# A decode step with attention and a gated MLP: 4 MB loads of keys and values in four large slots

## The chip, the cores and the metric

The kernel runs on one core of a Trainium2 chip. Five engines work side by side, each through its own list of instructions in order: TensorE (PE in the profile, its weight loads PEld), VectorE (DVE), ScalarE (ACT), GpSimd (POOL) and SyncE (SP). They meet only through semaphores. SBUF is the memory on the core, with 128 partitions; PSUM takes the results of matmuls. Sixteen DMA engines move data between HBM and SBUF; a load is issued by an engine, here nearly always SP, and is split into packets over the sixteen.

The metric is device time in microseconds of one execution. Before the change three runs gave 127.43 to 127.46 us, median 127.45.

## The reference

One token, a row x of 576 numbers, goes through two branches in parallel. x is layer-normalised first, and the result is x + A + B.

```python
# A: attention over the last W = 4096 positions of a cache of 65536
q = (xn @ wq)                      # 32 query heads of 128
k, v = k_cache[..., -W:, :], v_cache[..., -W:, :]   # 16 heads, each serves two query heads
p = softmax(q @ k.T * 128 ** -0.5)
A = (p @ v).reshape(1, 4096) @ wo
# B: gated MLP, sequence length 1
z = gelu(xn @ w_in)                # 4608
g = w_sp * layernorm(z[2304:]) + b_sp
B = (z[:2304] * g) @ w_out
```

All data are bfloat16. With one query row, nearly all of the work is to read memory: 33.6 MB of keys and values, and 4.7, 5.3, 2.7 and 4.7 MB of wq, w_in, w_out and wo: 50.96 MB.

## The kernel before, in words

**Loads.** All large loads are issued by SP, in the order of the program, into a ring of seven slots of 20736 bytes per partition (pool `ring`, L60; the loads L83, L90 and L95). There are 28: wq in three pieces of 1, 2 and 1.5 MB, w_in in three, eight loads of keys and eight of values, each for two heads (2 MB, 16 KB per partition, L90), w_out in one, wo in five (14, 9, 6, 2 and 1 rows per partition). A load into a used slot waits on SP until the last reader of the slot is done, and everything behind it on SP waits as well. Keys run two loads ahead of values.

**Layout of a key load.** A partition holds a run of consecutive positions of one head. For the scores q·k the 128 components of a key must lie along the partitions, so VectorE transposes 32x32 blocks of 32-bit words (`t_half`, L262, the transposes at L268) into a tile kT; one load is two halves of 2 transposes each. The blocks do not bring components alone onto the partitions but pairs of bf16 in a word and remainders of the position; the matmul takes out one component group at a time by reading kT with a step.

**Scores.** `s_half` (L271, matmul at L277) does 8 matmuls of 512 columns per half: for each of two heads four (`be` = 0 to 3) that accumulate in PSUM. Each head has its own tile position, a strip of 32 columns of the array, so matmuls of different positions can run at the same time. Within kT a head's successive columns lie 4 elements apart.

**Groups.** Four heads make a group; there are four groups. The loop at the end runs over 16 halves, four per group. In the last half of a group come `sm_a` (L296: maximum over the scores, spread over partitions, then two exponentials of 64 partitions x 1024 columns on ScalarE at L305) and pv of the group before (L338, matmul at L344: 32 matmuls of 512 columns over four positions). In the second half of the next group comes `sm_b` (L309: two transposes of the exponentials on VectorE at L315, sixteen copies of 32 x 64 words on ScalarE at L321 into the tile PT that pv reads). `norm` (L351), `y_mms` and `y_copy` turn the result of pv into four columns of Y; they follow one group later still. The MLP's `z_mms` (L375), gelu and layer norm are put between the halves of groups 0 and 1.

**The end.** After the loop: the last `sm_b`, pv, then 24 of the 36 matmuls with w_out, which need nothing of attention, then norm and Y of the last group, the other 12, and the 64 matmuls with wo (L467). A copy on VectorE and one on ScalarE and a small store end the kernel.

The order on every engine is that of the program: the kernel switches automatic scheduling off (L70), so an engine waits where an instruction stands that is not ready, even if a later one is. Semaphores for slots, PSUM tiles and buffers are put in by the framework.

Of the kernel before, what the change touches and what calls it, by code (L numbers as in the profile page):

```python
# [22 lines left out]
NT = W // 128  # L23
GK = 4
NG = HKV // GK
NP = HKV // 2
TP = 2 * NT
# [6 lines left out]
RING = 7  # L34
NS = 9
SLOT = NF * D
# [3 lines left out]
def kernel(  # L40
# [19 lines left out]
    ring = ctx.enter_context(tc.tile_pool(name="ring", bufs=RING))  # L60
    const = ctx.enter_context(tc.tile_pool(name="const", bufs=1))
    work = ctx.enter_context(tc.tile_pool(name="work", bufs=2))
    ktpool = ctx.enter_context(tc.tile_pool(name="ktpool", bufs=3))
# [11 lines left out]
    def ring_tile(name, rows, width):  # L75
        t = ring.tile([P, SLOT], BF16, name=name, tag="ring")
        return t[:, 0:rows * width].rearrange("p (s c) -> p s c", c=width)

    def load_halves(src, lo, n, name):

        v = ring_tile(f"{name}{lo}", n, src.shape[1] // 2)
        rows = src.rearrange("r (e c) -> (r e) c", e=2).rearrange("(p s) c -> p s c", s=NS)
        nc.sync.dma_start(v, rows[:, lo:lo + n, :])  # L83
        return [(lo + s, v[:, s, :]) for s in range(n)]

    def load_kv(src, m, name):

        t = ring.tile([P, SLOT], BF16, name=f"{name}{m}", tag="ring")
        v = t[:, 0:TP * DH]
        nc.sync.dma_start(v, src[0, 2 * m:2 * m + 2, SK - W:SK, :].rearrange("h (r t) d -> r h (t d)", t=TP))  # L90
        return v.rearrange("p (t d) -> p t d", d=DH)

    def load_n(src, per, lo, n, name):
        v = ring_tile(f"{name}{lo}", n, D)
        nc.sync.dma_start(v, src.rearrange("(p t) n -> p t n", t=per)[:, lo:lo + n, :])  # L95
        return [(lo + t, v[:, t, :]) for t in range(n)]

    K, V = {}, {}
    wq_sb = load_halves(A_wq, 0, 2, "wq") + load_halves(A_wq, 2, 4, "wq") + load_halves(A_wq, 6, 3, "wq")
    for m in range(2):  # L100
        K[m] = load_kv(A_k_cache, m, "k")
    win_sb = sum((load_halves(B_w_in, lo, 3, "win") for lo in (0, 3, 6)), [])
    for m in range(2, NP):
        K[m] = load_kv(A_k_cache, m, "k")
        V[m - 2] = load_kv(A_v_cache, m - 2, "v")
    for m in range(NP - 2, NP):
        V[m] = load_kv(A_v_cache, m, "v")
    wout_sb = load_n(B_w_out, NF, 0, NF, "wout")
    wo_sb = []
    for n in (14, 9, 6, 2, 1):  # L110
        wo_sb += load_n(A_wo, 32, len(wo_sb), n, "wo")
# [28 lines left out]
    idv = ident[:].rearrange("p (q c hh) -> p q c hh", q=4, hh=4)[:, :, 0:4, :]  # L140
    cm = const.tile([P, 4], FP32, name="cm")
    nc.vector.tensor_reduce(out=cm[:], in_=idv.rearrange("p q c hh -> p c q hh"), op=ALU.add,
                            axis=mybir.AxisListType.XY)
    dmask = const.tile([P, 4, DH], FP32, name="dmask")
    nc.gpsimd.tensor_copy(dmask[:], cm[:].unsqueeze(2).to_broadcast([P, 4, DH]))
    ohm = const.tile([P, 2, 4], FP32, name="ohm")
    for pr in range(2):
        nc.vector.tensor_reduce(out=ohm[:, pr, :], in_=idv[:, 2 * pr:2 * pr + 2].rearrange("p q c hh -> p hh q c"),
                                op=ALU.add, axis=mybir.AxisListType.XY)
# [3 lines left out]
    selv = sel[:].rearrange("p q (r hh e) -> p q r hh e", r=2, hh=4)  # L153
    for dq in range(4):
        nc.gpsimd.tensor_copy(selv[:, dq, :, :, dq], ohm[:])

    ids = ident[:].rearrange("p (i a h) -> p i a h", i=4, h=2)[:, :, 0:4, :]
    oha = const.tile([P, 4, 2], FP32, name="oha")
    nc.vector.reduce_sum(oha[:], ids.rearrange("p i a h -> p i h a"), axis=AXX)

    lsum = const.tile([P, 4, 8, 2, 2], FP32, name="lsum")
    nc.gpsimd.memset(lsum[:], 0.0)
    for hd in range(2):
        for pr in range(2):
            for th in range(2):
                nc.gpsimd.tensor_copy(lsum[:, 2 * pr + th, 0:4, hd, :],
                                      oha[:, 2 * hd + pr, :].unsqueeze(1).to_broadcast([P, 4, 2]))

    pz = []
    for n in range(2):  # L170
        t = const.tile([P, TP, 16, 2], BF16, name=f"pz{n}")
        nc.gpsimd.memset(t[:], 0.0)
        pz.append(t)
# [88 lines left out]
    def t_half(m, hf):  # L262

        kT = ktpool.tile([P, NT, 2, 16, 2, 2], BF16, name=f"kT{m}_{hf}", tag="kT")
        src = K[m][:, NT * hf:NT * (hf + 1), :].rearrange("p t d -> p (t d)").bitcast(FP32)
        dst = kT[:].rearrange("p t b r x e -> p (t b r x e)").bitcast(FP32)
        for n in range(2):
            nc.vector.transpose(dst[:, 1024 * n:1024 * (n + 1)], src[:, 1024 * n:1024 * (n + 1)])  # L268
        KT[m, hf] = kT

    def s_half(m, hf):  # L271
        g, pr = divmod(m, 2)
        kv = KT.pop((m, hf))[:].rearrange("p t b r x e -> p b e x t r")
        for hd in range(2):
            i = 2 * hd + pr
            for be in range(4):
                nc.tensor.matmul(  # L277
                    S[g % 2][32 * i:32 * i + 8, hf, :],
                    lhsT=Qb[:, 2 * m + hd, be].rearrange("p a h -> p (a h)"),
                    rhs=kv[:, be // 2, be % 2, hd],  # L280
                    start=(be == 0), stop=(be == 3), tile_position=(0, 32 * i),
                )
# [13 lines left out]
    def sm_a(g):  # L296
        s = S[g % 2]
        nc.vector.tensor_reduce(out=mx[:, 0:1], in_=s[:], op=ALU.max, axis=mybir.AxisListType.XY)  # L298
        bk = spread(mx, mb, g, ALU.max, "m")
        nm = work.tile([P, 1], FP32, name=f"nm{g}", tag="nm")  # L300
        nc.vector.tensor_scalar_mul(nm[:], bk[:, 0:1], -SCALE)  # L301
        p = pz[g % 2]
        for hd in range(2):
            lo, hi = 64 * hd, 64 * hd + 64
            nc.scalar.activation(p[lo:hi, :, :, hd], s[lo:hi].rearrange("p a (t r) -> p (a t) r", r=16), ACT.Exp,  # L305
                                 bias=nm[lo:hi, 0:1], scale=SCALE, accum_out=lx[lo:hi, g:g + 1])
        st[g] = {"p": p}

    def sm_b(g):  # L309
        d = st[g]  # L310
        pt = work.tile([P, TP, 32], BF16, name=f"pt{g}", tag="pt")
        src = d["p"][:].rearrange("p t r x -> p (t r x)")
        dst = pt[:].rearrange("p t x -> p (t x)")
        for n in range(2):
            nc.vector.transpose(dst[:, 1024 * n:1024 * (n + 1)], src[:, 1024 * n:1024 * (n + 1)])  # L315
        PT = work.tile([P, 2, TP, 2, 2], BF16, name=f"PT{g}", tag="PT")
        pt4 = pt[:].rearrange("p t x -> p (t x)").bitcast(FP32).rearrange("p (t x) -> p t x", x=16)
        PT4 = PT[:].rearrange("p r t x h -> p (r t x h)").bitcast(FP32).rearrange("p (r t x) -> p r x t", r=2, x=2)
        for i in range(GK):
            for a in range(4):  # L320
                nc.scalar.copy(PT4[32 * a:32 * a + 32, i % 2, i // 2, :], pt4[32 * i:32 * i + 32, :, a])  # L321
        d["PT"] = PT

    def sums(g):

        lps = ps_m.tile([P, 32], FP32, name=f"lps{g}", tag="m")
        nc.tensor.matmul(lps[:, 0:1], lhsT=lsum[:].rearrange("p q c x h -> p (q c x h)"), rhs=lx[:, g:g + 1],  # L327
# [10 lines left out]
    def pv(g):  # L338

        d = st[g]  # L340
        for tb in range(NT // 4):
            for q in range(4):
                pr, t0 = q // 2, NT * (q % 2) + 4 * tb
                nc.tensor.matmul(  # L344
                    ops[32 * q:32 * q + 16, :],
                    lhsT=d["PT"][:, pr, t0:t0 + 4].rearrange("p t x h -> p (t x h)"),
                    rhs=V[2 * g + pr][:, t0:t0 + 4, :],
                    start=(tb == 0), stop=(tb == NT // 4 - 1), tile_position=(0, 32 * q),
# [79 lines left out]

    for j in range(2 * NP):
        g, o = divmod(j, GK)  # L430
        t_half(j // 2, j % 2)
        if o == 3:
            if g > 0:
                recip(g - 1)
            if g > 1:
                norm(g - 2)
        s_half(j // 2, j % 2)
        if g > 0 and o == 1:
            if g > 1:
                sm_b(g - 1)  # L440
            else:
                G, sz = z_gelu(*z_exp(zps))

                acc = []
                for n, pool in enumerate((ps_a, ps_b)):
                    t = pool.tile([P, 512], FP32, name=f"acc{n}", tag="ab"[n])
                    acc.append(t[32 * n:32 * n + 1, 0:CW])
                    nc.tensor.matmul(acc[n], lhsT=ones_b[:, 0:1], rhs=xrow[:, CW * n:CW * (n + 1)],
                                     start=True, stop=False, tile_position=(0, 32 * n))
                hv = z_norm(G, sz)  # L450
        if g > 0 and o == 2:
            sums(g - 1)
        if o == 3:
            if g > 1:
                y_mms(g - 2)
            sm_a(g)
            if g > 1:
# [67 lines left out]
```

## Time and profile before

| what | value |
|---|---|
| median of 3 runs | 127.45 us (127.43 to 127.46) |
| span of the profiled execution | 125.4 us; no other time of that execution is given |
| TensorE busy | 68.4 us in 626 matmuls |
| VectorE busy | 78.5 us in 150 instructions |
| ScalarE busy | 33.6 us in 85 instructions |
| GpSimd busy | 7.9 us |
| moved by DMA | 51.06 MB in 4047 packets, 407 GB/s over the span |

The page cuts the span into 40 slices of about 3.1 us and gives, for each engine, the busy tenth of each slice, the clock that TensorE was granted (5 is half speed), and the busy share of the DMA engines. The chain that ended last is followed back from the last instruction to whatever released each wait. A group's line has the source line, engine, operation, output<-input with their shapes, the count, and then busy time, mean ns of one, and the idle time of the engine before it with what ended it. A line of the timeline has start, duration, engine, line, operation and count. Durations of overlapping matmuls are longer than the distance of their starts; where matmuls at four positions overlap, the distance is what counts.

### The profile page before, as it was taken

What the parts mean: (1) busy time and instruction counts of PE and PEld (TensorE: products, weight loads), DVE (VectorE), ACT (ScalarE), POOL (GpSimd) and SP (SyncE); (2) the same over time, 40 slices, a digit from 0 to 9 for tenths busy, and PEclk for the clock granted to TensorE, in tenths of its full rate; (3) what the DMA queues carried; (4) which work ended last, traced back from release to release, by engine and by line L of the source; (5) the groups of instructions that cost most, each with busy time, mean ns of one, the idle gap of its engine ahead of it and who ended that gap; (6) DMA issues with size and microseconds to landing.
All of it is one profiled execution on the core that took longest, in us unless ns stands there. A gap on an engine that the chain in (4) does not pass through costs nothing.

```text
span 125.4 us, 1630 instructions
## 1 busy us (share of the span) xinstructions
PE 68.4 (55%) x626; PEld 31.4 (25%) x626; DVE 78.5 (63%) x150; ACT 33.6 (27%) x85; POOL 7.9 (6%) x27
## 2 busy tenths in 40 slices
PE   0034810398999668069257049639029811178862
PEld 0021110112699612014011012411003511024640
DVE  6853049997517595794798298899098967005001
ACT  4000030000072950000441940260860092920001
POOL 2991000000000000100000000000000000000000
PEclk9999995558975555959958977986955996557998
DMA  4999999999999999999999999999999999999960
GB/s 115 455 423 422 425 434 439 422 428 435 428 438 418 434 434 428 423 444 423 428 439 434 413 439 434 428 428 434 428 436 434 428 426 439 434 409 427 416 261 0
DMA packets 4047, 51.06 MB, mean 407 GB/s; under 512 B 454, under 2 KB 584, under 8 KB 840
## 3 DMA queue, kind: packets, MB, share of 16 engines
q1 hardware_dynamic: 4032, 50.96, 95.6%
q8 instruction: 5, 0.08, 0.2%
q14 instruction: 2, 0.02, 0.0%
q10 hardware_dynamic: 8, 0.00, 0.0%
HBM read 50.96 MB, written 0.00 MB: 406 GB/s over the span
## 4 chain that ended last, share of the span: by engine, by line
DMA 71%; PE 11%; DVE 11%; issue 2%; SPq 1%; ACT 1%
DMA k<-in_A_k_cache_dram 44%; DMA wo<-in_A_wo_dram 17%; DMA wq<-in_A_wq_dram 10%; DVE kT L268 6%; PE S L277 5%; PE ops L344 3%; DVE Qb L255 2%; PE qps L227 1%; PE acc L467 1%; DVE q_rep L238 1%; ACT q_rep L236 1%; DVE on L358 1%; PE lps L327 1%; SPq L83 1%; DVE om L354 1%
## 5 line engine op out<-in xcount | busy, mean ns | idle before, releaser
L277 PE MATMUL S<-kT,Qb 128*8 128x512 bf16 x128 | 32.3, 636 | 30.3 <-DVE kT L268 30.3
L268 DVE STREAM_TRANSPOSE kT<-k 128x1024 f32<-128x1024 f32 x32 | 36.9, 1212 | 8.3 <-DMA k<-in_A_k_cache_dram 8.3
L305 ACT ACTIVATE pz<-S,nm 64x1024 bf16<-64x1024 f32 x8 | 11.2, 1406 | 45.0 <-DVE nm L301 30.3
L321 ACT COPY PT<-pt 32x64 f32<-32x64 f32 x64 | 18.9, 295 | 14.6 <-DVE pt L315 13.8
L277 PEld LDWEIGHTS <-Qb 128*8 128x8 bf16 x128 | 6.4, 96 | 49.7 <-issue 46.7
L344 PE MATMUL ops<-v,PT 128*16 128x512 bf16 x128 | 11.7, 441 | 3.5 <-ACT PT L321 3.5
L315 DVE STREAM_TRANSPOSE pt<-pz 128x1024 bf16<-128x1024 bf16 x8 | 9.4, 1212 | 4.1 <-ACT pz L305 4.1
L380 PEld LDWEIGHTS <-win 128*128 128x128 bf16 x162 | 10.1, 165 | 0.9 <-issue 0.9
L380 PE MATMUL zps<-XT,win 128*128 128x2 bf16 x162 | 10.2, 201 | 0.0
L354 DVE SCALAR_TENSOR_TENSOR om<-ops,rs,dmask 128x512 f32<-128x512 f32 x4 | 3.0, 742 | 7.4 <-PE ops L344 7.3
L298 DVE TENSOR_REDUCE mx<-S 128x1 f32<-128x1024 f32 x4 | 4.9, 1220 | 3.7 <-PE S L277 3.7
L344 PEld LDWEIGHTS <-PT 128*16 128x16 bf16 x128 | 5.0, 97 | 7.3 <-ACT PT L321 4.1
L227 PE MATMUL qps<-wq,XT 128*2 128x512 bf16 x36 | 4.2, 621 | 2.3 <-DVE XT L218 1.9
L467 PE MATMUL acc<-wo,Y 128*1 128x288 bf16 x64 | 4.6, 285 | 1.3 <-DMA wo<-in_A_wo_dram 1.3
L236 ACT CAST q_rep<-qps 128x512 bf16<-128x512 f32 x2 | 1.2, 585 | 14.0 <-DVE q_rep L238 14.0
L238 DVE CAST q_rep<-qps 128x512 bf16<-128x512 f32 x2 | 1.4, 692 | 5.1 <-PE qps L227 4.5
L193 PE MATMUL ps_x<-ones_b,xtw 1*128 1x1 bf16 x9 | 0.4, 162 | 7.2 <-DVE xtw L191 7.2
L492 DVE CAST res<-acc 1x288 bf16<-1x288 f32 x1 | 0.4, 446 | 6.1 <-PE acc L467 6.1
L358 DVE TENSOR_REDUCE on<-om 128x128 f32<-128x512 f32 x4 | 4.1, 1034 | 0.1
L327 PE MATMUL lps<-lx,lsum 128*128 128x1 f32 x8 | 2.1, 333 | 3.2 <-DVE Y L372 3.2
L493 ACT CAST res<-acc 1x288 bf16<-1x288 f32 x1 | 0.4, 389 | 12.4 <-PE acc L467 12.4
L467 PEld LDWEIGHTS <-Y 128*1 128x1 bf16 x64 | 2.9, 83 | 3.0 <-issue 1.9
(90 smaller groups left out, 46.8 us busy)
## 6 DMA issues: line engine op xcount, KB each, us to landing
k<-in_A_k_cache_dram SPq DMA_DIRECT2D x8, 2048.0 KB, 27.2
v<-in_A_v_cache_dram SPq DMA_DIRECT2D x8, 2048.0 KB, 27.8
win<-in_B_w_in_dram SPq DMA_DIRECT2D x3, 1728.0 KB, 27.1
wout<-in_B_w_out_dram SPq DMA_DIRECT2D x1, 2592.0 KB, 30.2
wq<-in_A_wq_dram SPq DMA_DIRECT2D x1, 2048.0 KB, 9.3
wo<-in_A_wo_dram SPq DMA_DIRECT2D x1, 2016.0 KB
wq<-in_A_wq_dram SPq DMA_DIRECT2D x1, 1536.0 KB, 12.5
wo<-in_A_wo_dram SPq DMA_DIRECT2D x1, 1296.0 KB
```

The source lines that it names most:

```text
L227: nc.tensor.matmul(qps[32 * g:32 * g + 2, :], lhsT=XT[:, s, :], rhs=wv[:, 512 * g:512 * (g + 1)], start=(s == 0), stop=(s == NS - 1), tile ...
L268: nc.vector.transpose(dst[:, 1024 * n:1024 * (n + 1)], src[:, 1024 * n:1024 * (n + 1)])
L277: nc.tensor.matmul(S[g % 2][32 * i:32 * i + 8, hf, :], lhsT=Qb[:, 2 * m + hd, be].rearrange("p a h -> p (a h)"), rhs=kv[:, be // 2, be % 2 ...
L298: nc.vector.tensor_reduce(out=mx[:, 0:1], in_=s[:], op=ALU.max, axis=mybir.AxisListType.XY)
L305: nc.scalar.activation(p[lo:hi, :, :, hd], s[lo:hi].rearrange("p a (t r) -> p (a t) r", r=16), ACT.Exp, bias=nm[lo:hi, 0:1], scale=SCALE, ...
L315: nc.vector.transpose(dst[:, 1024 * n:1024 * (n + 1)], src[:, 1024 * n:1024 * (n + 1)])
L321: nc.scalar.copy(PT4[32 * a:32 * a + 32, i % 2, i // 2, :], pt4[32 * i:32 * i + 32, :, a])
L344: nc.tensor.matmul(ops[32 * q:32 * q + 16, :], lhsT=d["PT"][:, pr, t0:t0 + 4].rearrange("p t x h -> p (t x h)"), rhs=V[2 * g + pr][:, t0:t ...
L354: nc.vector.scalar_tensor_tensor(out=om[:].rearrange("p c d -> p (c d)"), in0=ops[:], scalar=d["rs"][:, 0:1], in1=dmask[:].rearrange("p c ...
L358: nc.vector.reduce_sum(on[:], om[:].rearrange("p c d -> p d c"), axis=AXX)
L380: nc.tensor.matmul(zps[:, :, t], lhsT=wt[:, t, :], rhs=XT[:, s, :], start=(s == 0 and t == 0), stop=(s == NS - 1 and t == NF - 1), skip_gr ...
L467: nc.tensor.matmul(acc[n], lhsT=lhs[:, col:col + 1], rhs=wv[:, CW * n:CW * (n + 1)], start=False, stop=last, tile_position=(0, 32 * n))
```

## The change

Keys and values come four heads at a time, a whole group in one load of 4 MB, 32 KB per partition. There are 17 loads instead of 28, into four slots named a, b, c and d of 32 KB per partition, plus a small one, f, for the last row of wo. The order of the loads on SP is wq (8 of its 9 rows per partition), wq's last row, K0, w_in (7 of 9), w_in's last two, K1, K2, V0, K3, V1, V2, V3, w_out, wo in 18, 10, 3 and 1 rows. Which slot each takes is written in the calls.

With four heads in a load, a chunk (`keys`, `scores`) is half of a group: four transposes, then 16 matmuls of 512 columns over four tile positions. Within kT a head's successive columns now lie 8 elements apart. The exponentials are four per group, each of 32 partitions x 1024 columns. The transposes of the exponentials work on 32-bit words, and the sixteen copies move 32 x 128 words each. The tiles pz and pt have one buffer instead of two. The order of the work is written as a sequence of calls: pv, norm and Y of a group follow directly after one another (`tail`), one group after its exponentials, and all 36 matmuls with w_out stand after the last `tail`.

```diff
-RING = 7
 NS = 9
-SLOT = NF * D
...
+    def load_kv(slot, src, g, name):
+
+        t = big.tile([P, TP * DH], BF16, name=f"{name}{g}", tag=slot)
+        nc.sync.dma_start(t[:], src[0, GK * g:GK * g + GK, SK - W:SK, :].rearrange("h (r t) d -> r h (t d)", t=TP))
+        return t[:].rearrange("p (t d) -> p t d", d=DH)
...
+    rest = big.tile([P, TP * DH], BF16, name="rest", tag="d")
+    wq_sb = rows("a", wq_h, "wq", 0, 8) + rows(rest, wq_h, "wq", 8, 1, 0)
+    K[0] = load_kv("b", A_k_cache, 0, "k")
+    win_sb = rows("c", win_h, "win", 0, 7) + rows(rest, win_h, "win", 7, 2, 2048)
+    K[1] = load_kv("a", A_k_cache, 1, "k")
+    K[2] = load_kv("b", A_k_cache, 2, "k")
+    V[0] = load_kv("c", A_v_cache, 0, "v")
+    K[3] = load_kv("d", A_k_cache, 3, "k")
+    V[1] = load_kv("a", A_v_cache, 1, "v")
+    V[2] = load_kv("b", A_v_cache, 2, "v")
+    V[3] = load_kv("c", A_v_cache, 3, "v")
+    wout_sb = rows("a", B_w_out, "wout", 0, NF)
+    wo_sb = (rows("d", A_wo, "wo", 0, 18) + rows("b", A_wo, "wo", 18, 10)
+             + rows("c", A_wo, "wo", 28, 3) + rows("f", A_wo, "wo", 31, 1))
...
-        kT = ktpool.tile([P, NT, 2, 16, 2, 2], BF16, name=f"kT{m}_{hf}", tag="kT")
+        kT = ktpool.tile([P, TC, 2, 8, GK, 2], BF16, name=f"kT{g}_{c}", tag="kT")
...
+    def scores(g, c):
+        kv = KT.pop((g, c))[:].rearrange("p t b r x e -> p b e x t r")
+        for be in range(4):
+            for x in range(GK):
                 nc.tensor.matmul(
+                    S[g % 2][32 * x:32 * x + 8, c, :],
+                    lhsT=Qb[:, GK * g + x, be].rearrange("p a h -> p (a h)"),
+                    rhs=kv[:, be // 2, be % 2, x],
+                    start=(be == 0), stop=(be == 3), tile_position=(0, 32 * x),
                 )
...
+        pv_ = pz[:].rearrange("p t r x e -> p t e r x")
+        for x in range(GK):
+            lo, hi = 32 * x, 32 * x + 32
+            nc.scalar.activation(pv_[lo:hi, :, :, :, x], s[lo:hi].rearrange("p a (t e r) -> p (a t) e r", e=2, r=8),
+                                 ACT.Exp, bias=nm[lo:hi, 0:1], scale=SCALE, accum_out=lx[lo:hi, g:g + 1])
...
-                nc.scalar.copy(PT4[32 * a:32 * a + 32, i % 2, i // 2, :], pt4[32 * i:32 * i + 32, :, a])
+                nc.scalar.copy(PT4[32 * a:32 * a + 32, :, x, :], pt[32 * x:32 * x + 32, :, 2 * a:2 * a + 2])
...
+    def group(g, between):
+        keys(g, 0)
+        scores(g, 0)
+        between()
+        keys(g, 1)
+        scores(g, 1)
+        sm_a(g)
+
+    group(0, lambda: None)
+    zps = z_mms()
+    sm_b(0)
+    zg = []
+    group(1, lambda: zg.extend(z_exp(zps)))
+    G, sz = z_gelu(*zg)
...
+    hv = z_norm(G, sz)
+    sums(0)
+    group(2, lambda: sm_b(1))
+    pv(0)
+    tail(0)
+    sums(1)
+    group(3, lambda: sm_b(2))
+    pv(1)
+    tail(1)
+    sums(2)
+    sm_b(3)
+    pv(2)
+    tail(2)
+    sums(3)
+    pv(3)
...
+    tail(3)
+    for c in range(3):
+        out_hv(c)
     for t, wv in wo_sb:
         out_mms(Y, t, wv, t == 31)
```

`tail(g)` is recip, norm, y_mms and y_copy of group g; `rows` loads a number of rows of a matrix into a slot.

## The prediction

> **What bounds the kernel now.** I read the strip of slices and the chain that ended last, then the transfers, then the timeline of the last 25 us, then the rates of single instructions.
>
> ```profile
> span 125.4 us, 1630 instructions
> ...
> DMA  4999999999999999999999999999999999999960
> ...
> DMA 71%; PE 11%; DVE 11%; issue 2%; SPq 1%; ACT 1%
> ...
> wo<-in_A_wo_dram SPq DMA_DIRECT2D x1, 144.0 KB, 8.7
> ```
>
> All 16 DMA engines are busy from slice 1 to slice 38, and 71% of the chain is transfers. So the reader should see a kernel bound by its 50.96 MB. The third wq load is issued at 1.62 us and lands 12.45 us later (the chain's piece "DMA wq"), after 4.72 MB. The last load is issued at 113.88 and lands 8.7 us later, at 122.6, after 50.96 MB. Between them lie 46.24 MB in 108.5 us, 426 GB/s, and a load that ends at X MB lands at 3.0 + X/0.426 us. The three runs have a median of 127.45 us; of the profiled execution only the span is given, so 2.05 us is taken to lie around it.
>
> How late is the arithmetic behind that? The timeline of the last group:
>
> ```profile
> 100.32 1.40 ACT L305 ACTIVATE pz<-S,nm 64x1024 bf16<-64x1024 f32 x1 [7.30 <-PE ops L344]
> ...
> 101.79 1.39 ACT L305 ACTIVATE pz<-S,nm 64x1024 bf16<-64x1024 f32 x1
> ...
> 103.26 2.37 DVE L315 STREAM_TRANSPOSE pt<-pz 128x1024 bf16<-128x1024 bf16 x2 [1.00 <-ACT pz L305]
> ...
> 105.72 4.90 ACT L321 COPY PT<-pt 32x64 f32<-32x64 f32 x16 [2.49 <-DVE pt L315]
> ...
> 110.67 3.59 PE L344 MATMUL ops<-v,PT 128*16 128x512 bf16 x30 [0.64 <-ACT PT L321]
> ...
> 116.64 0.20 DVE L372 CAST Y<-yps 32x32 bf16<-32x32 f32 x1 [0.53 <-PE yps L365]
> ...
> 121.53 1.42 PE L467 MATMUL acc<-wo,Y 128*1 128x288 bf16 x18 [0.80 <-DMA wo<-in_A_wo_dram]
> ```
>
> Y is ready at 116.84 and needs 64 matmuls of about 0.07 us (28 took 1.88): 121.4 without any load. The arithmetic is only some 1.5 us ahead of the transfers. A change that delays its last group by more becomes slower, whatever it does for the loads.
>
> Last, what a strided read costs on TensorE:
>
> ```profile
> 76.32 1.98 PE L277 MATMUL S<-kT,Qb 128*8 128x512 bf16 x8
> ...
> 78.83 1.89 PE L344 MATMUL ops<-v,PT 128*16 128x512 bf16 x29
> ...
> L380 PEld LDWEIGHTS <-win 128*128 128x128 bf16 x162 | 10.1, 165 | 0.9 <-issue 0.9
> ...
> L244 PEld LDWEIGHTS <-q_rep 98*128 98x128 bf16 x16 | 0.5, 96 | 3.7 <-ACT q_rep L236 3.7
> ```
>
> Eight score matmuls take about 2 us. Their records start in pairs (two tile positions at once) every 0.43 to 0.47 us, at 67.3 and 77.2 with the granted clock at 1.00 just as at 45 with it at 0.50. The pv matmuls read V in one piece and start four at a time every 0.216 us at clock 1.00, every 0.427 at 0.50. So the scores are held by their reading: they take every fourth bf16 of kT, 8 bytes apart. The win weights, 36 bytes apart, load in 165 ns where contiguous ones take 96.
>
> **Transfers, all edits of loads together.** By the packet records a packet of 16384 bytes takes 611 ns, one of 20736 771, one of 1152 51: 36.8 ns per KB (1000 bytes) and 9 ns each. A 32 KB packet is then about 1213 ns against 2 x 611. Each engine has 64 such pairs in K and V (0.57 us), saves about 0.17 in wq, win and wo, and 11 completion packets of 9 ns: 0.84 us in all. Bounds: 0 to 0.84. It counts only if transfers still set the end.
>
> **SP's queue.** Loads go out in order, each behind its slot's last reader. With landings K0 23.9, K1 46.2, K2 56.1, V0 65.9, K3 75.8, V1 85.6, V2 95.4, V3 105.3 and the schedule below: K2 waits for the transposes of K0 (33.1, the ring is full to 46), V0 for the win matmuls (44.7, full to 56), V1 for K1's transposes (57.8, full to 76), V2 for K2's (79.7, full to 86), V3 for pv(0) (86.5, full to 95). wout waits for pv(1), about 108, and the ring ran out at 105; wo18 stands behind it. The gap of some 5 us (2.3 us from issue to first bytes, as wq's first load shows, included) is covered by the arithmetic, which wants wout only at 126.6. wo3 waits for pv(3), 124.2, and lands at about 127.5, before its matmuls at 133.
>
> **Arithmetic.** The transposes stay 40 of 1.2 us and the score and pv matmuls 128 each; what changes is the grouping and the order on DVE. New or resized:
> - Exponentials go from 2 per group (64 partitions x 1024) to 4 (32 x 1024). The time follows the free size (64x1024 1406 ns, 128x512 cast 585), so the pitch of 1.47 us stays: 5.9 for 2.9, +3.0 per group. Their writes now step 16 bytes; low end 1.47, high end 2.0 (the weight loads' 67 ns extra on 128 elements, carried to 1024: 0.54). I take 1.47, the nearest row's.
> - PT copies move 128 elements, not 64: 295 ns + 64 x 0.42 (from the casts of 64 and 288 elements) and the gap of 11: 0.333, 5.3 per group. Ends 0.306 and 0.6.
> - A score chunk is 16 matmuls over four positions, four each, as now four each over two. Today the last transpose ends at 56.66 and the maximum starts at 58.82: 2.16 us, of which 4 x 0.45 is matmuls. The new kT has four heads side by side, so a head's columns are 16 bytes apart. Low end: no change, 2.15 (below it: 1.22 if the reads stop being the limit, 4 x 0.216). High end: the rate is shared among the readers, two readers 0.45, four readers twice the step, 7.5. The row at 8 bytes costs double the contiguous one at full clock and the row at 36 bytes (62 ns between weight loads against 26) more than double, so I take the time as growing with the step: 0.9 per matmul, 3.95 per chunk.
>
> The Trainium skill bears on this row ("SBUF — State Buffer", Specifications): SBUF lines have 16 bytes, and a reader needs two or more hits in a line for full bandwidth. By it the 8-byte step was the last with two hits and the new one pays, and the sum is near 138.7; but the same page of the skill (in "Door 1: The DMA port swizzle") calls a stride of up to 8 bf16 elements free, and by that the sum is 131.8. The trace fits both so far: the 8-byte step has 0.45 us at either clock, and no run here shows the 16-byte one.
>
> **The sum** is a chain on DVE, with nobody else to fill its waits, since the order is written out:
> - K0 lands 23.9 (Qb is done by 23.0: wq's first load lands at 12.8, 36 matmuls 4.05, then 6.1 as between 15.59 and 21.69). Eight transposes 9.15, scores 3.95, maximum and spread 2.3 (58.82 to 61.13), exponentials 6.0, pt 2.4: 47.7. K1 has landed (46.2).
> - Group 1: transposes 4.6, gelu start 0.85, transposes 4.6, scores 3.95, spread 2.3, gelu and norm 4.1 (47.90 to 52.00): 68.1.
> - Group 2: 4.6, pt 2.35, 4.6, scores 3.95, 2.3, wait for pv(0) and sums 0.6, om to Y 2.5 (114.30 to 116.84): 89.0.
> - Group 3: 4.6 + 2.35 + 4.6 + 3.95 + 2.3: 106.8. Today this point is 100.2.
> - Tail: exponentials 6.0, pt 2.4, copies 5.4, pv 3.6 (granted clock 0.50 there, 1.95 at 1.00), to Y 2.5: 126.7. Today 24 of the 36 wout matmuls lie under DVE's part of this tail; now all come after it: 3.0 (24 took 2.04), wo 4.5: 134.2. From the last matmul to the end 2.45 as now (122.95 to 125.4): span 136.7, time **138.7**, +11.3 us.
>
> pz and pt now have one buffer each: the exponentials of a group wait for the pt transposes of the group before, which are done 11 us earlier (75.1 against 86 for group 2), so the wait costs nothing; if pt(g) came after the maximum of g+1, its 2.4 would be added per group. The preamble's edits (fewer small constants on DVE and POOL) lie before K0's landing and cost nothing.
>
> **Rivals.**
> - The 16-byte step costs nothing (2.15 per chunk). Three chunks give back 5.4 and the start moves to K1's landing, 1.5: **131.8**. For it: 0.45 per 512 columns may be one element per read whatever the step. Against: the weight loads at 36 bytes. 0.26.
> - The step also slows the exponentials' writes, or four readers collide. 0.54 more on each exponential is 2.2 per group, and the first and the last group show it: **143**. Readers that share one rate (7.5 per chunk) would add 3.55 to four chunks: 153. Against: nothing shows such writes, and two scores and two pv matmuls ran side by side at 57.2 to 58.1 without a slower rhythm (0.44). 0.17.
> - Not slower: the limit on scores goes away with four positions, and TensorE runs all its bursts at full pace. From 131.8: chunks 1.22, 2.8 less; pv(3) 1.95 for 3.6; wout and wo at 0.07 throughout, 0.5; pv(0) 0.2: **126.7**, and transfers, 0.84 shorter, would end at 126.6. It decides once the last matmul is done by 122.9. Against: the pair rhythm at clock 1.00. 0.04.
>
> **Numbers.** My forecast has 0.53. Its own range is 136 to 142 (copies, clock of the last burst, step between 0.8 and 1.0). The 8-in-10 range takes in the first rival and the lower part of the second: 131 to 146. Within 0.2% is what a measurement here can't tell from no change. Faster 0.03 and same 0.01 come from the last rival, slower 0.96 from all else.
>
> **What would show it.** Strip: DMA no longer 9 to the end, a gap near 105 to 111. Waits: wout's issue on SP for pv(1). Score records: four starts together, then 0.9 us (0.45 would be the first rival). Exponentials of group 3 starting near 107, Y near 127, 100 final matmuls after it. Packets of 32 KB at 1.21 us. Wrong if the chain still ends in "DMA wo" with PE idle before it.

## The result: 187.24 us, 47% slower

The changed kernel takes 187.24 us (186.99 to 187.65) against 127.46 us; the ratio is 1.468, 95% interval 1.467 to 1.470. The forecast was slower, at 138.7 us, with a range of 131 to 146. The direction was right and the size was not.

The page of the changed kernel: the line of the span, busy times, the strip of the DMA engines, the chain that ended last, and three groups.

```profile
span 185.9 us, 1619 instructions
...
PE 67.9 (37%) x626; PEld 29.6 (16%) x626; DVE 78.6 (42%) x150; ACT 99.3 (53%) x101; POOL 7.1 (4%) x19
...
DMA  6999999999999999990000399980002999400400
...
ACT 44%; DVE 26%; PE 15%; DMA 12%; issue 1%; SPq 0%; ACTq 0%
...
L289 ACT ACTIVATE pz<-S,nm 32x1024 bf16<-32x1024 f32 x16 | 76.6, 4787 | 42.2 <-DVE nm L285 19.6
L261 PE MATMUL S<-kT,Qb 128*8 128x512 bf16 x128 | 30.8, 1079 | 68.2 <-DVE kT L254 68.2
...
L300 DVE STREAM_TRANSPOSE pt<-pz 128x1024 f32<-128x1024 f32 x8 | 9.5, 1224 | 59.0 <-ACT pz L289 59.0
```

Look first at ScalarE: 99.3 us busy where it was 33.6. The sixteen exponentials take 4787 ns each; before, eight took 1406. VectorE stands idle for 59.0 us before the pt transposes, always for the exponentials. The chain is 44% ScalarE and 12% transfers; it was 71% transfers. The strip keeps its 9s until slice 17 and then has three holes: the loads wait for slots, whose last readers the exponentials hold back.

The order of the last group, from the chain:

```profile
136.57 3.92 PE S L261 x9
140.51 1.23 DVE mx L282
...
142.94 4.86 ACT pz L289 x2
147.81 4.75 ACT pz L289 x2
152.57 4.74 ACT pz L289 x2
157.33 4.75 ACT pz L289 x2
162.10 2.38 DVE pt L300 x2
...
169.66 3.63 PE ops L326 x32
...
175.81 7.43 PE acc L456 x98
183.24 0.43 DVE res L470
```

A score chunk, from the last transpose to the maximum, is 3.9 us, as the prediction had it (3.95). The exponentials from 142.94 to 162.10 are 19.2 us where the prediction had 6.0. From there to the end it goes as forecast: pt 2.4, copies, pv 3.6, the final matmuls 7.4.

Put 19.3 us for the four exponentials, the mean of the four groups (19.2 to 19.4), into the prediction's own sum. Groups 0 and 3 wait for all of them: 13.3 more each. In group 1 the sum has 4.1 for gelu and norm and 4.6 for four transposes meanwhile, which cover 8.7 us, so 10.6 more; in group 2 it has 0.6, 2.5 and 4.6, which cover 7.7, so 11.6 more. Together 48.8, and 138.7 becomes 187.5, against 187.24 measured. So one term accounts for the miss. What makes an exponential cost 4.8 us was then the question.

### The profile page after: what moved, and what is told of

It is laid out like the page before. It is cut to its first block, busy times and chain, and to the rows that moved or that the text cites. A ratio compares the mean times of both kernels' runs of the same rounds, so it can differ in the third digit from the quotient of the medians.

```text
span 185.9 us, 1619 instructions
## 1 busy us (share of the span) xinstructions
PE 67.9 (37%) x626; PEld 29.6 (16%) x626; DVE 78.6 (42%) x150; ACT 99.3 (53%) x101; POOL 7.1 (4%) x19
## 4 chain that ended last, share of the span: by engine, by line
ACT 44%; DVE 26%; PE 15%; DMA 12%; issue 1%; SPq 0%; ACTq 0%
ACT pz L289 41%; DVE kT L254 15%; DMA k<-in_A_k_cache_dram 12%; PE S L261 8%; DVE pt L300 5%; PE acc L456 4%; DVE mx L282 3%; ACT PT L303 3%; PE ops L326 2%; DVE on L340 1%; DVE mb L277 0%; DVE mt L271 0%; SPq L81 0%; DVE om L336 0%; DVE mb L274 0%
## 5 line engine op out<-in xcount | busy, mean ns | idle before, releaser
L289 ACT ACTIVATE pz<-S,nm 32x1024 bf16<-32x1024 f32 x16 | 76.6, 4787 | 42.2 <-DVE nm L285 19.6
L300 DVE STREAM_TRANSPOSE pt<-pz 128x1024 f32<-128x1024 f32 x8 | 9.5, 1224 | 59.0 <-ACT pz L289 59.0
L303 ACT COPY PT<-pt 32x128 f32<-32x128 f32 x64 | 19.6, 306 | 10.6 <-DVE pt L300 9.9
L261 PEld LDWEIGHTS <-Qb 128*8 128x8 bf16 x128 | 3.9, 94 | 87.8 <-issue 84.9
L326 PE MATMUL ops<-v,PT 128*32 128x512 bf16 x128 | 9.8, 455 | 1.3 <-ACT PT L303 1.3
L362 PEld LDWEIGHTS <-win 128*128 128x128 bf16 x126 | 7.9, 164 | 1.8 <-issue 1.8
L362 PE MATMUL zps<-XT,win 128*128 128x2 bf16 x126 | 8.0, 202 | 0.0
L289 ACT ACTIVATION_READ_ACCUMULATOR pz<-S,nm 32x1 f32 x16 | 7.8, 487 | 0.0
L326 PEld LDWEIGHTS <-PT 128*32 128x32 bf16 x128 | 4.8, 112 | 7.3 <-issue 4.5
L340 DVE TENSOR_REDUCE on<-om 128x128 f32<-128x512 f32 x4 | 4.1, 1024 | 0.1
L456 PE MATMUL acc<-wout,hv 128*1 128x288 bf16 x36 | 3.9, 397 | 0.0
```

What stands on the lines that cost most here:

```text
L261: nc.tensor.matmul(S[g % 2][32 * x:32 * x + 8, c, :], lhsT=Qb[:, GK * g + x, be].rearrange("p a h -> p (a h)"), rhs=kv[:, be // 2, be % 2, x],
L289: nc.scalar.activation(pv_[lo:hi, :, :, :, x], s[lo:hi].rearrange("p a (t e r) -> p (a t) e r", e=2, r=8), ACT.Exp, bias=nm[lo:hi, 0:1], s ...
L303: nc.scalar.copy(PT4[32 * a:32 * a + 32, :, x, :], pt[32 * x:32 * x + 32, :, 2 * a:2 * a + 2])
L326: nc.tensor.matmul(ops[32 * q:32 * q + 32, :], lhsT=d["PT"][:, t0 // 2:t0 // 2 + 2].rearrange("p t x h e -> p (t x h e)"), rhs=V[g][:, t0: ...
L340: nc.vector.reduce_sum(on[:], om[:].rearrange("p c d -> p d c"), axis=AXX)
L362: nc.tensor.matmul(zps[:, :, t], lhsT=wt[:, t, :], rhs=XT[:, s, :], start=(s == 0 and t == 0), stop=(s == NS - 1 and t == NF - 1), skip_gr ...
```

## The experiments

### Results side by side

```diff
-            nc.scalar.activation(pv_[lo:hi, :, :, :, x], s[lo:hi].rearrange("p a (t e r) -> p (a t) e r", e=2, r=8),
+            nc.scalar.activation(pf[lo:hi, 0:1024], s[lo:hi].rearrange("p a c -> p (a c)"),
```

> The changed kernel, with one thing different: each exponential writes its 1024 results side by side at the start of its rows of pz and not at their places (16 bytes apart), so the attention weights are misplaced; all waits stay as they are. Theory W (where the results are written costs the time): each exponential falls from 4.79 us to about 1.4, the chain of the prediction holds again with its measured score chunks of 3.9 us, and the time is 137 to 140 us. Rival F (the form costs it: 32 partitions, four instructions per group, the accumulated sum): the exponentials stay at 4.8 us and the time at 187 us. Rival S (another edit also carries part of the loss, for instance the strided scores or the transfers): exponentials of 1.4 us and a time above 145 us.

Measured: 134.99 us, ratio to the kernel before 1.061 (1.054 to 1.067). The group in this run:

```profile
L290 ACT ACTIVATE pz<-S,nm 32x1024 bf16<-32x1024 f32 x16 | 17.7, 1106 | 42.4 <-DVE nm L285 20.2 <-DVE rs L317 11.3 <-DVE th L381 10.6
```

1106 ns with the same 32 partitions, the same four instructions per group and the same accumulated sum: the form is not to blame, the place of the results is, and 52 of the 60 us go with it. The time is 2 us under the range that was given, because the exponentials come at a distance of 1.22 us and not 1.47, which groups 0 and 3 both show (1.0 us less in each), and the final matmuls ran in 6.05 us and not 7.5.

### Two ladders of exponentials

Each exponential of one kernel writes with another pattern, each on a line of its own. Each ladder ran once, and only its profile is used: a pattern has two instructions there. The first ladder, with the calls of the last six patterns left out and comments put in for their names:

```diff
+            if g % 2 == 0 and x == 0:    # side by side
+                nc.scalar.activation(pf[lo:hi, 0:1024], s[lo:hi].rearrange("p a c -> p (a c)"),
...
+            elif g % 2 == 0 and x == 1:  # 4 bytes apart
+                nc.scalar.activation(pf[lo:hi, 0:2048].rearrange("p (c s) -> p c s", s=2)[:, :, 0], ...
+            elif g % 2 == 0 and x == 2:  # two passes, 16 bytes apart
...
+            elif g % 2 == 0 and x == 3:  # word by word, 16 bytes from word to word
...
+            elif g % 2 == 1 and x == 0:  # 8 bytes apart
...
+            elif g % 2 == 1 and x == 1:  # 16 bytes apart, 512 columns
...
+            elif g % 2 == 1 and x == 2:  # own order
...
+            elif g % 2 == 1 and x == 3:  # runs of 8, 4 bytes apart, with jumps
...
```

> The changed kernel, with each exponential writing in another order, so that one profile holds a ladder; in three of the eight forms the results land at their right places, in the others they are misplaced, and one form takes only 512 columns. Groups 0 and 2: side by side; 4 bytes apart; 16 bytes apart in two passes over all places (low halves of the words, then high halves); the two halves of a word one after the other, words 16 bytes apart. Groups 1 and 3: 8 bytes apart; 16 bytes apart with 512 columns; the changed kernel's own order (runs of 8 results 16 bytes apart, then the same 8 words again for their other halves); runs of 8 results 4 bytes apart, with jumps. Theory W1 (every result written 16 bytes or more from the last costs about 4.5 ns): the two passes take 4.8 us, 512 columns 2.5 us, word by word 2.5 us, own order 4.8 us, the runs at 4 bytes 1.5 us. Theory W2 (coming back to the same words within 8 results costs it): two passes 1.4 to 1.6 us, 512 columns 0.8 us, own order 4.8 us, word by word 4.8 us or more. Theory W3 (short runs cost it): the runs at 4 bytes take 4.8 us, two passes 1.4 us.

The groups of that run, one line of the kernel per pattern. L291 is side by side, L294 4 bytes, L297 two passes, L300 word by word, L303 8 bytes, L306 16 bytes with 512 columns, L309 the changed kernel's own order, L312 the runs (groups of other instructions left out):

```profile
L297 ACT ACTIVATE pz<-S,nm 32x1024 bf16<-32x1024 f32 x2 | 9.8, 4920 | 0.1
L309 ACT ACTIVATE pz<-S,nm 32x1024 bf16<-32x1024 f32 x2 | 9.6, 4802 | 0.1
L306 ACT ACTIVATE pz<-S,nm 32x512 bf16<-32x512 f32 x2 | 5.1, 2544 | 0.1
L303 ACT ACTIVATE pz<-S,nm 32x1024 bf16<-32x1024 f32 x2 | 5.1, 2528 | 16.4 <-DVE th L403 10.7 <-DVE rs L339 5.7
L294 ACT ACTIVATE pz<-S,nm 32x1024 bf16<-32x1024 f32 x2 | 2.8, 1416 | 0.1
L312 ACT ACTIVATE pz<-S,nm 32x1024 bf16<-32x1024 f32 x2 | 2.7, 1367 | 0.1
L300 ACT ACTIVATE pz<-S,nm 32x1024 bf16<-32x1024 f32 x2 | 2.4, 1183 | 0.1
L291 ACT ACTIVATE pz<-S,nm 32x1024 bf16<-32x1024 f32 x2 | 2.2, 1105 | 25.5 <-DVE nm L285 19.8 <-DVE rs L339 5.8
```

Coming back to the same words (W2) falls: two passes, where a word is met again only after 512 results, cost as much as the own order. Short runs (W3) fall: L312. W1 fits but for one line: word by word was to take 2.5 us and takes 1.18, while it enters as many stretches of 16 bytes (512) as the line with 512 columns. So a pair that fills a word is handled differently from a single half.

The second ladder was made to tell step from size; its calls are shown without their ends, and the comments give the lines of the kernel:

```diff
+        pw = pwt[:]   # scratch tile of 32-bit words
...
+                nc.scalar.activation(pf[lo:hi].rearrange("p (c s) -> p c s", s=8)[:, :, 0:2], ...           # L292
+                nc.scalar.activation(pf[lo:hi].rearrange("p (c e s) -> p c e s", e=4, s=2)[:, :, 0:2, 0], ... # L295
+                nc.scalar.activation(pf[lo:hi, 0:3072].rearrange("p (c s) -> p c s", s=3)[:, :, 0], ...       # L298
+                nc.scalar.activation(pw[lo:hi].rearrange("p (c s) -> p c s", s=4)[:, :, 0], s[lo:hi, 0, 0:256], # L301
+                nc.scalar.activation(pw[lo:hi, 0:1024], ...                                                   # L304
+                nc.scalar.activation(pw[lo:hi].rearrange("p (c s) -> p c s", s=2)[:, :, 0], s[lo:hi, 0, :],    # L307
+                nc.scalar.activation(pf[lo:hi, 0:1024], s[lo:hi].rearrange("p a (t e r) -> p (a t) r e", e=2, r=8), # L310
+                nc.scalar.activation(pf[lo:hi].rearrange("p (c s) -> p c s", s=16)[:, :, 0], s[lo:hi, 0, 0:256], # L313
```

> The changed kernel with a second ladder of exponentials; results are misplaced, some forms take only part of the columns, and some write 32-bit results into a scratch tile. Groups 0 and 2: pairs side by side with 16 bytes from pair to pair, read from PSUM in order; pairs 4 bytes apart with 16 bytes from pair to pair; single results 6 bytes apart; 32-bit results 16 bytes apart, 256 columns. Groups 1 and 3: 32-bit results side by side; 32-bit results 8 bytes apart, 512 columns; 16-bit results side by side, read from PSUM in the order of words; single 16-bit results 32 bytes apart, 256 columns. Theory I (the innermost step sets the cost, about 1.15 ns per 4 bytes stepped, whatever the size of a result): 1.2, 1.4, 1.8, 1.4 us; 1.4, 1.4, 1.2, 2.5 us. Theory L (a single result in a new 16-byte stretch costs about 4.5 ns, and no more for 32 bytes): 1.2, 1.4, 1.8, 1.4 us; 1.2 to 1.4, 1.4, 1.2, 1.4 us. Theory H (only half-word results cost it): 32-bit results at 16 bytes take 0.5 us.

```profile
L295 ACT ACTIVATE pz<-S,nm 32x1024 bf16<-32x1024 f32 x2 | 5.2, 2588 | 0.0
L298 ACT ACTIVATE pz<-S,nm 32x1024 bf16<-32x1024 f32 x2 | 4.0, 1988 | 0.0
L313 ACT ACTIVATE pz<-S,nm 32x256 bf16<-32x256 f32 x2 | 2.8, 1376 | 0.0
L292 ACT ACTIVATE pz<-S,nm 32x1024 bf16<-32x1024 f32 x2 | 2.4, 1194 | 25.9 <-DVE nm L286 20.3 <-DVE rs L340 5.7
L304 ACT ACTIVATE pwt<-S,nm 32x1024 f32<-32x1024 f32 x2 | 2.2, 1105 | 16.3 <-DVE th L404 10.6 <-DVE rs L340 5.7
L310 ACT ACTIVATE pz<-S,nm 32x1024 bf16<-32x1024 f32 x2 | 2.2, 1105 | 0.0
L301 ACT ACTIVATE pwt<-S,nm 32x256 f32<-32x256 f32 x2 | 1.5, 732 | 0.1
L307 ACT ACTIVATE pwt<-S,nm 32x512 f32<-32x512 f32 x2 | 1.4, 713 | 0.0
```

Theory I falls at L313: 32 bytes apart costs per result what 16 bytes cost. Theory L missed three lines: L295, where pairs 4 bytes apart were to take 1.4 us and took 2.6, and the two of 32-bit results with a step, L301 and L307, which were to take 1.4 us each and took half of it. H, that only half words cost it, holds only in part: L301 was to take 0.5 us and took 0.73. All sixteen patterns fit one count, which was made after the runs. From L306 and L313 (512 results in 2544 ns, 256 in 1376) an exponential has about 208 ns of its own and then 4.56 ns per single result. Divide what is left of each line by the number of 16-byte stretches that it enters: 4.5 to 4.7 ns per stretch at steps of 4, 6, 8, 16 and 32 bytes, for L295, for the runs and for the own order, all written in single halves of words; 1.9 to 2.1 ns for whole words (L292, L301, L307). Below that a pace of 0.88 ns per result binds, that of the results side by side (L291, L304 and L310, 1105 ns). L310 reads PSUM in the order of words and costs nothing more, so the reading has no part in it. Why halves cost more than double is not shown by these runs.

### The order mended

```diff
-            nc.scalar.activation(pv_[lo:hi, :, :, :, x], s[lo:hi].rearrange("p a (t e r) -> p (a t) e r", e=2, r=8),
+            nc.scalar.activation(pz[lo:hi, :, :, x, :], s[lo:hi].rearrange("p a (t e r) -> p (a t) r e", e=2, r=8),
```

> The changed kernel with the exponentials' order alone different: position, then word, then the two halves of the word innermost, so each result lies next to the one before or 16 bytes after a pair; every result still lands where the changed kernel puts it. In the ladder this form took 1.18 us. Theory W (the order of writing is the whole surplus): the time is that of results side by side, 134 to 136 us. Rival (with useful values in place something else appears, such as the strided reads of PSUM slowing the maximum or the accumulated sum): over 138 us.

Measured: 135.41 us, ratio 1.062 (1.056 to 1.069), the same as with results side by side. Two subscripts, the same values in the same places, and 51.8 of the 59.8 us are gone.

### What a strided read costs the scores

```diff
+        step = {(0, 0): 1, (0, 1): 2, (1, 0): 4, (1, 1): 4, (2, 0): 8, (2, 1): 16, (3, 0): 16, (3, 1): 8}[g, c]
...
-                    rhs=kv[:, be // 2, be % 2, x],
+                    rhs=kf[:, 0:512 * step].rearrange("p (n s) -> p n s", s=step)[:, :, (x * 2 + be) % step],
```

> As the run with results side by side, and each chunk of scores reads its 512 columns of kT with another step (the scores are of wrong columns): 2, 4, 8, 8, 16, 32, 32, 16 bytes for the eight chunks in order. Theory of the prediction (time grows with the step): a round of four matmuls takes 0.22 to 0.43 us at 2 bytes (by the granted clock), about 0.45 at 8, 0.88 at 16, and 1.8 at 32. Rival (a read costs one amount up to 8 bytes and double from 16 on): 0.45 at 4 and 8, 0.88 at 16 and at 32. Rival (four positions share one reading rate): 0.9 at 8 bytes with four positions, where the kernel before has 0.45 with two.

This kernel ran once as well. The timeline of TensorE, one line per chunk of 16 matmuls (other lines left out), with steps of 2, 4, 8, 8, 16, 32, 32 and 16 bytes:

```profile
25.45 1.88 PE L263 MATMUL S<-kT,Qb 128*8 128x512 bf16 x16 [4.81 <-DVE kT L254]
29.95 1.88 PE L263 MATMUL S<-kT,Qb 128*8 128x512 bf16 x16 [2.63 <-DVE kT L254]
48.58 1.98 PE L263 MATMUL S<-kT,Qb 128*8 128x512 bf16 x16 [3.70 <-DVE kT L254]
53.86 1.98 PE L263 MATMUL S<-kT,Qb 128*8 128x512 bf16 x16 [3.31 <-DVE kT L254]
65.67 3.77 PE L263 MATMUL S<-kT,Qb 128*8 128x512 bf16 x16 [3.71 <-DVE kT L254]
74.68 3.84 PE L263 MATMUL S<-kT,Qb 128*8 128x512 bf16 x16 [5.25 <-DVE kT L254]
88.50 3.84 PE L263 MATMUL S<-kT,Qb 128*8 128x512 bf16 x16 [3.88 <-DVE kT L254]
93.00 3.79 PE L263 MATMUL S<-kT,Qb 128*8 128x512 bf16 x16 [0.67 <-DVE kT L254]
```

Rounds of four matmuls start 0.37 to 0.45 us apart up to 8 bytes and 0.88 to 0.92 at 16 and at 32. The second theory holds from 8 bytes on: double at 16, and no more at 32. The prediction's reason (time grows with the step) gave the right price at 16 and would have been wrong at 32. Four positions at 8 bytes keep the rhythm that two had before, so readers do not share.

The first two chunks have to be read with care. The trace has no record of the granted clock before 52.5 us, so the clock of the chunks with 2 and 4 bytes is not known. Their rounds are mostly 0.42 to 0.43 us apart, as those of the contiguous pv matmuls in the kernel before are at a clock of 0.50 (0.427); at 1.00 these are 0.216 us apart. The second chunk with 8 bytes, at 53.86, ran at a recorded 1.00 and still took 0.44, so 8 bytes cost about double there; what 2 and 4 bytes would cost at 1.00 is not shown. At 16 bytes the price is the same at 0.50 (65.67) and at 1.00 (the last chunk from 93.88 on); 32 bytes were seen at 0.50 alone.

The Trainium skill ("SBUF — State Buffer", Specifications) asks for two or more hits in a line of 16 bytes for full bandwidth. The step from 0.44 to 0.9 us between 8 and 16 bytes agrees with it; that 8 bytes, with two hits, take 0.44 and not 0.216 at a clock of 1.00 does not. The remark of the Trainium skill (the same page, "Door 1: The DMA port swizzle") that a stride of 8 bf16 elements is free does not agree either: these 16 bytes took 0.9.

Both mended, with the scores reading side by side as well:

```diff
-                    rhs=kv[:, be // 2, be % 2, x],
+                    rhs=kf[:, 2048 * x + 512 * be:2048 * x + 512 * be + 512],
```

> As the run with results side by side, and the scores too read their 512 columns side by side (wrong columns). By the prediction's chain with chunks of 1.4 to 2.1 us: 128 to 132 us, so still slower than before, by the four exponentials per group (3.0 us in the tail) and by the w_out matmuls behind the last norm. Rival (the strided accesses are all that is wrong with the change): 126.6 us, the transfers' end.

Measured: 130.34 us, ratio 1.022 (1.020 to 1.024). The strided scores are worth 4.65 us (134.99 less 130.34). With both accesses side by side, what is left of the change still loses 2.2%: the order of the work, the four exponentials for two, and the loads, which this run does not tell apart. The expectation's chain had 128 to 132.

### The order of the work

The next kernels have the mended order of the exponentials and the strided scores, and each keeps the last one's edits. First, 24 of the w_out matmuls before the last norm:

```diff
-    tail(3)
-    for c in range(3):
-        out_hv(c)
+    recip(3)
+    out_hv(0)
+    out_hv(1)
+    norm(3)
+    y_mms(3)
+    y_copy(3)
+    out_hv(2)
```

> The same with 24 of the 36 w_out matmuls put between pv of the last group and its norm, as in the kernel before. The prediction's tail says that they cost 3.0 us behind the norm; VectorE's part of the tail takes 2.5 us, so 2.0 to 2.5 us come back: 132 to 133 us. Rival (TensorE's clock, not the order, sets the tail): less than 1 us.

Measured: 133.23 us, ratio 1.045 (1.044 to 1.047), 2.2 us less. Next, transposes ahead of the maximum:

```diff
+    def half(g, c):
+        keys(g, c)
+        scores(g, c)
...
+    half(1, 1)
+    half(2, 0)
+    sm_a(1)
...
+    sm_b(1)
+    half(2, 1)
+    half(3, 0)
+    sm_a(2)
+    pv(0)
+    tail(0)
+    sums(1)
+    half(3, 1)
+    sm_b(2)
+    sm_a(3)
```

> The same again, and the first transposes of the next group of keys put ahead of the maximum of this group (groups 1 to 2 and 2 to 3), so that VectorE works while TensorE does the strided scores; the gelu and norm of the MLP stay where they are. Theory of the prediction (a chain on VectorE whose waits nobody fills sets the end, not the transfers): two waits of 3.9 us are filled, the last exponentials start near 97 us and the transfers, 0.84 us shorter by their larger packets, set the end: 126.6 us, up to 127.5 if the last load's matmuls trail. Rival (the larger loads themselves stand in the way: slots come free too late and the queue runs dry): above 130 us, with holes in the transfers.

Measured: 128.92 us, ratio 1.011 (1.009 to 1.013). 4.3 us came back, and VectorE's waits for scores fell to 5.6 us in all. The last exponentials started at 101.28 and not near 97: VectorE waited 3.3 us for pv of group 0, which stood behind a score chunk on TensorE, and ScalarE's exponentials stood 1.3 us behind its own copies of group 2. The rival falls, since the transfers ran without a hole (9 or 8 in every full slice). Then pv is put first:

```diff
     half(2, 1)
+    pv(0)
     half(3, 0)
     sm_a(2)
-    pv(0)
     tail(0)
```

> The pipelined kernel, with the pv matmuls of group 0 put ahead of the first score chunk of group 3 on TensorE, so that VectorE's norm does not wait behind that chunk (3.3 us idle before om at 86.7). Theory (the arithmetic chain still sets the end by about 1.5 us, the transfers stand right behind it): the last exponentials start 3 us earlier, the end falls onto the transfers, 127.2 to 127.8 us. Rival (the chain is bound elsewhere): no change, 128.9 us.

Measured: 127.45 us beside 127.27 us, ratio 1.0014 (1.0005 to 1.0022). So with 17 loads in four slots of 32 KB, the exponentials' order and the work's order mended, the kernel is within 0.2% of the one with 28 loads. The loads themselves cost no more than that.

The next two were meant to show whether the transfers are all that is left. Half of the copies go to GpSimd, and then the wo load of 10 rows is split as well:

```diff
+                if a % 2:
+                    nc.gpsimd.tensor_copy(PT4[32 * a:32 * a + 32, :, x, :], pt[32 * x:32 * x + 32, :, 2 * a:2 * a + 2])
+                else:
+                    nc.scalar.copy(PT4[32 * a:32 * a + 32, :, x, :], pt[32 * x:32 * x + 32, :, 2 * a:2 * a + 2])
```

> The same, and half of the sixteen PT copies of a group on GpSimd. The tail loses some 2.5 us more of arithmetic. Theory (the transfers now set the end, and larger packets bring little: the pipelined kernel's last load landed at 122.43 us against 122.62): no more than 0.3 us below the run with pv early, 127.2 to 127.5 us, the same as before. Rival (the packet records' 0.84 us comes out once the queue never runs dry): 126.6 us.

```diff
+    wob = big.tile([P, 10 * D], BF16, name="wob", tag="b")
+    wo_sb = wo_sb + rows(wob, A_wo, "wo", 18, 6, 0) + rows(wob, A_wo, "wo", 24, 4, 6 * D)
```

> The same, and the wo load of 10 rows per partition split into 6 and 4 in the same slot, so that after its landing 8 matmuls are left and not 20. If the transfers set the end: 0.5 to 0.8 us less than with 10 rows, 126.6 to 126.9 us. If the arithmetic does: no change.

Measured: 128.54 us, ratio 1.009 (1.008 to 1.011), and 128.06 us, ratio 1.0055 (1.004 to 1.007). Both expectations failed. The arithmetic was done 2.6 us sooner (the w_out matmuls end at 115.05 us and not at 117.70), and the kernel got slower. The split took some 0.5 us off, as forecast, but from a level that lay over 1 us too high. Windows of TensorE, first with copies on GpSimd, then with pv early alone (us of the span, length, busy and matmuls, granted clock, DMA share, GB/s):

```profile
115.00:117.00 2.00, 0.05 (x2) 1.00 0.93 397
...
118.00:119.00 1.00, 1.00 (x18) 0.80 0.93 395
119.00:120.00 1.00, 1.00 (x12) 0.50 0.92 379
120.00:121.00 1.00, 1.00 (x12) 0.50 0.71 268
121.00:122.00 1.00, 1.00 (x12) 0.50 0.26 100
```

```profile
115.00:117.00 2.00, 1.83 (x34) 0.95 0.95 403
...
118.00:119.00 1.00, 1.00 (x20) 1.00 0.94 397
119.00:120.00 1.00, 1.00 (x20) 1.00 1.00 412
```

The wo matmuls in the timelines of the same two runs, in the same order:

```profile
117.81 5.76 PE L472 MATMUL acc<-wo,Y 128*1 128x288 bf16 x64 [2.77 <-DMA wo<-in_A_wo_dram]
```

```profile
117.84 2.37 PE L469 MATMUL acc<-wo,Y 128*1 128x288 bf16 x36
...
121.31 1.88 PE L469 MATMUL acc<-wo,Y 128*1 128x288 bf16 x28 [1.10 <-DMA wo<-in_A_wo_dram]
```

In the first, TensorE had nothing to do from 115.05 to 117.81, since wo had not landed. Its clock was 0.50 from 118.6 to 122.0, and the 64 wo matmuls took 5.76 us and ended at 123.57. In the second it was busy until then, kept 1.00, paused 1.1 us for wo and still ended at 123.19. So the clock is worth about 0.4 us; that the pause brought it is read from its place and was not tested alone. But the span is 0.9 us longer, 126.7 against 125.9. The other 0.5 us lies behind the last matmul: from there to the end of the span it is 3.16 us with copies on GpSimd and 2.67 without, and in the records of the trace it is GpSimd's drain at the end of the program that ends later, 0.54 us after the other engines' semaphores and not 0.06. Why the copies lengthen it is not shown. Then the split was tried without the copies on GpSimd:

> The kernel with pv early, PT copies on ScalarE alone, and the wo load of 10 rows per partition split into 6 and 4. TensorE arrives at the wo matmuls late enough not to idle before them. Theory (what made the two runs with copies on GpSimd slower is TensorE's clock after its idle time, 0.50 from 118.8 to 122): here the clock stays at 1.00 through the wo matmuls, the last landing leaves 8 matmuls and not 28, and the time is 0.2 to 0.4 us below the run with pv early, at or just under the kernel before. Rival (the split itself, one more load, costs it): no less than with pv early.

Measured: 127.22 us beside 127.31 us, ratio 0.9993 (0.9984 to 1.0002), with the clock at 1.00 in every window from 117 to 123 and 2.61 us from the last matmul to the end. So the split itself does not cost the time. This run takes both away at once, the slow clock and GpSimd's late end, so it does not tell them apart; their sizes are those read from the two traces above. Against the run with pv early the split helps by 0.2%, and the kernel ends level with the one before. No version beat it.

## Why the prediction was right and wrong, point by point

- **Bound now, and the 1.5 us of room.** Right: from a kernel bound by transfers, every version with a longer arithmetic chain was slower.
- **The exponentials: the step that failed.** "Low end 1.47, high end 2.0 ... I take 1.47, the nearest row's." Measured 4.8 us from one to the next, 19.2 to 19.4 for the four. The changed write step was seen, and even a rival was made of it, at 0.17 and 143 us, but it was priced with TensorE's weight loads. Those are reads of another engine, and they bound nothing for ScalarE's writes. The term should have been left open at the top, and the rival would then have had a range far above 146.
- **Score chunks.** 3.95 forecast, 3.9 to 4.0 measured; the reading rule behind it was wrong beyond 16 bytes, so the right price was in part luck. The first rival (no effect of 16 bytes) falls.
- **The chain on VectorE with waits that nobody fills.** Right: with the exponentials' measured time it gives 187.5 for 187.24, and filling the waits brought 4.3 us.
- **The tail.** 3.0 us for the w_out matmuls behind the norm was forecast as their price; putting 24 of them ahead brought 2.2.
- **PT copies.** 0.333 forecast, 0.306 each and 0.315 apart measured.
- **SP's queue.** A hole near 105 was forecast, where w_out waits for pv of group 1. That one came at 127.6 to 143.5 us (w_out was issued at 142.54), and two more came: at 85.7 to 105.4, where V2 waited for the last transposes of K2 until 104.03, and at 161.7 to 174.3, where the last rows of wo waited for pv of group 3 until 173.31. All three readers stood behind exponentials. The holes cost nothing by themselves, as said: the chain that ended last has no load in it but K0, and with the order mended the queue kept ahead. After a hole the first packet started 1.0 to 1.3 us after the issue, where the prediction had 2.3; nothing hung on it.
- **Transfers.** The 32 KB packets took 1213 ns, the number forecast. But the 0.84 us that this should save did not come out: by the semaphore events the last load landed at 122.62 us in the kernel before and at 122.50, 122.67 and 122.61 in the pipelined kernel, with pv early and with copies on GpSimd, and the last load of values at 105.4 to 105.6 against 105.4. Where it goes is open.
- **The rival on the other side** (126.7: with four positions the limit on scores goes away) falls: four positions at 8 bytes keep 0.44 us, and the kernel takes 130.3 even with both accesses side by side.

## What to carry to other kernels

When an edit changes the step of an access, ask for each engine that reads or writes it, and take no price from another engine or from reads for writes: without a row of that kind the upper end is open. Let the innermost index of a 16-bit result fill whole words; here the order of two indices was 52 us. And before moving work off a wait, look at what the freed engine waits for next, the clock of TensorE included, and at what the engine that takes the work adds at the end.

## What the runs showed of the hardware that was not expected

- A ScalarE exponential that writes single 16-bit results pays 4.5 to 4.7 ns for each 16-byte stretch it enters, at steps from 4 to 32 bytes; whole words pay 1.9 to 2.1 ns, at 8 and 16 bytes. So the kernel before already paid: 1406 ns at 4 bytes against 1105 side by side.
- A matmul's moving operand of 512 bf16 columns, read with a step of 8 bytes, takes 0.41 to 0.47 us at a granted clock of 1.00 as at 0.50, and 0.84 to 0.94 with 16 bytes at either; read in one piece it takes 0.216 and 0.427. At 32 bytes it took no more than at 16 (0.89 to 0.92, clock 0.50).
- In the run with copies on GpSimd TensorE had no matmul for 2.8 us just before the last burst, and its granted clock was 0.50 from 118.6 to 122.0; without that pause it stayed at 1.00. The burst ended 0.4 us later. The kernel before shows the same in its middle: no matmul from 80.7 to 83.6 us, and a clock of 0.50 from 83.7 to 87.1.
